# A gated SSM and GEGLU kernel: the sequence transform as 64 by 32 on 64-row TensorE tiles, new scratch layouts, and a fixed order table

## The chip, the cores and the metric

One core of a Trainium2 chip. The metric is device microseconds for one execution. Medians are over all runs of a kernel, ratios over its fast-state runs alone. A "span" is the length of the one execution that was profiled; it is about 2 us below the time. A run is called slow, and left out of the ratios, when it is over 1.5% above the fastest of its kernel. In the profiles PE is TensorE, PEld its weight loads, DVE the vector engine, ACT the scalar engine, POOL GpSimd, SP the engine that issues the transfers and SPq its queue; L851 is line 851 of the kernel in question.

## The reference

Input u is [1, 2048, 640] in bf16. The output mixes a long convolution with a feed-forward network (FFN) by a gate per position:

```python
# branch A: for each of 640 channels a filter K of 2048 taps from 128 complex modes, applied by FFT
P = exp(dt*A * l);  K = einsum("dn,dnl,dn->dl", C, P, dt*B).real
Yf = rfft(pad(u)) * rfft(pad(K));  a = irfft(Yf)[..., :2048] + u * Dskip
# branch B
b = (gelu(x @ w_gate) * (x @ w_up)) @ w_down        # 640 -> 1728 -> 640
g = sigmoid((x * gate_w).sum(-1))
return g * a + (1 - g) * b
```

## The kernel before

The 640 channels are worked in two halves, 0 and 1, of W = 320. For each half the kernel makes tables of the modes (sines on ACT, products on DVE), contracts them to K (TensorE), writes K to DRAM (`dS`), gathers it back (`Kl`), and runs a two-step transform of K and of u, with a trip through DRAM between the steps (`dU`, `dKA`). Spectra are multiplied, transformed back (`dY`), and the last step meets the FFN's result (`zt`).

A complex product needs a second copy `Us` of the spectrum `U`, with real and imaginary rows exchanged. The partitions 0 to 63 hold the real rows, so the exchange is two transfers of contiguous halves:

```python
arena = mp.tile([128, ARENA // 2], BF16, name="arena")     # ONE SBUF tensor for nearly everything;
v = arena[:, off // 2:(off + size) // 2]                   # every buffer is a view of it
...
def u_spec(h, R):
    for c in range(4):
        ks = stageB(dU[h], ..., U[c], ...)
        for s in range(2):
            dma(320, lambda c=c, s=s: nc.sync.dma_start(out=Us[c][64*s:64*s+64], in_=U[c][64-64*s:128-64*s]), r=ks, ...)
def chain(h, R):
    for c in range(4):
        ...                                                # K spectrum -> t
        ve(... U[c]  = U[c]  * t)
        ve(... Us[c] = Us[c] * t)
```

Work is recorded as steps with the data that they read and write; a list scheduler (`plan.run()`) picks engine and order from a cost model. Every engine then has its own list in that order. The waits between engines are not written in the kernel: the recording layer adds them, from the areas that the instructions touch.

Of the kernel before, what the change touches and what calls it, by code (L numbers as in the profile page):

```python
# [12 lines left out]
I32 = mybir.dt.int32  # L13
# [8 lines left out]
X2 = [1, 2, 3, 4, 5, 6, 7, 8, 258, 260, 262, 264, 516, 520, 772, 776, 1032, 1288, 1544, 1800]  # L22
NE = len(X2)


class Plan:
# [50 lines left out]
    def run(self):  # L77
        S = self.steps
        left = [len(s["deps"]) for s in S]
        succ = [[] for _ in S]  # L80
        for s in S:
            for d in s["deps"]:
                succ[d].append(s["i"])
        free, done, aset, line = {}, {}, None, 0
        cand = {}
        ready = {}
        pairs = [0.0] * 4
        owner = {}
        last = None
        warm, cols, wend = False, 0, 3413  # L90

        def arrive(i):
            s = S[i]
            for e in s["engs"]:
                t = 0
                for d in s["deps"]:
                    same = S[d]["eng"] == e and not S[d]["x"]
                    t = max(t, done[d] + (0 if same else S[d]["lat"]))
                ready[i, e] = t
                cand.setdefault(e, set()).add(i)  # L100

        for s in S:
            if not s["deps"]:
                arrive(s["i"])
        order = []
        INF = 1e18
        while len(order) < len(S):
            best = None
            for e, c in cand.items():
                if not c:  # L110
                    continue
                pmin = min(pairs) if e == "PE" else 0
                m = min((max(ready[i, e], pmin) if S[i]["psum"] else ready[i, e]) for i in c)
                t = max(m, free.get(e, 0))
                if best is None or t < best[0]:
                    best = (t, e, pmin)
            t, e, pmin = best
            assert t < INF, "deadlock"
            pick = None
            for i in cand[e]:  # L120
                s = S[i]
                rd = max(ready[i, e], pmin) if s["psum"] else ready[i, e]
                if rd > t:
                    continue
                sc = s["rank"] - s["age"] * (t - ready[i, e]) / 1000
                if s["aset"] not in (None, aset) and e == "ACT":
                    sc += self.switch
                if pick is None or (sc, i) < pick:
                    pick = (sc, i)
            s = S[pick[1]]  # L130
            i = s["i"]
            for e2 in s["engs"]:
                cand[e2].discard(i)
            s["eng"] = e
            s["t"] = t
            ns = s["engs"][e]
            if e == "ACT" and s["aset"] not in (None, aset):
                ns += 1280
                aset = s["aset"]
            if e == "DVE" and last in s["deps"]:  # L140
                ns += 60
            if e == "DVE":
                last = i
            if s["psum"]:
                p = min(range(4), key=lambda q: (pairs[q], q))
                s["k"] = 2 * p
                pairs[p] = INF
                owner[i] = p
            if e == "PE":
                while t >= wend:  # L150
                    warm = cols >= 3072
                    cols = 0
                    wend += 3413
                    if t >= wend + 3413:
                        warm, wend = False, t - t % 3413 + 3413
                rest, ns = ns, 0
                while rest > 0:
                    rate = 1 if warm else 0.5
                    room = wend - t - ns
                    step = min(rest, room * rate)  # L160
                    cols += s["cr"] * step
                    rest -= step
                    ns += step / rate
                    if rest > 0:
                        warm, cols, wend = cols >= 3072, 0, wend + 3413
            free[e] = done[i] = t + ns
            if s["x"]:
                line = max(line, t + ns) + s["x"]
                done[i] = line
            if s["frees"] is not None:  # L170
                f = S[s["frees"]]
                if all(d in done for d in f["rel"]):
                    pairs[owner[f["i"]]] = max(done[d] for d in f["rel"]) + 150
            order.append(s)
            for d in succ[i]:
                left[d] -= 1
                if not left[d]:
                    arrive(d)
        self.order = sorted(order, key=lambda s: (s["t"], s["i"]))
        self.done = done  # L180
        return max(done.values())

    def emit(self):
        for s in self.order:
            s["fn"](s)
# [3 lines left out]
def kernel(  # L189
# [26 lines left out]
    out3 = out.rearrange("b (m p) d -> (b m) p d", p=NPH)  # L216
# [5 lines left out]
    ARENA = 212224  # L222
    arena = mp.tile([128, ARENA // 2], BF16, name="arena")
    ps = pp.tile([128, 8, 512], FP32, name="ps")
    P = dict(sw=5.4, gate=1.91, up=2.5, gelu=8.59, age=0.75, mul=-0.94, un=1.65, uw=1.85, K0=2.33, K1=5.9,
             W=6.08, RT=6.44, ua=0.33, ue=6.48, down=2.99, z=2.89, T2=2.96, A0=6.55, U0=-3.8, A1=2.03, C0=-4.3,
             F0=0.78, U1=1.3, C1=1.89, F1=0.8)
    plan = Plan(P["sw"])
    add = plan.add
# [30 lines left out]
    def mm(n):  # L260
        return n / 2.4 + 4
# [10 lines left out]
    def dma(kb, fn, r=(), w=(), rank=5.0, **k):  # L272
        return add({"SP": 450}, lambda s: fn(), r, w, rank=rank, lat=1900, x=max(100, kb * 3.2), **k)
# [31 lines left out]
    O_TB = O_W + 5120  # L305
    O_WA = O_TB + 768
    O_CS1 = O_WA + 8192
    O_CS2 = O_CS1 + 40960
    O_TRIG = O_CS2 + 25600
    O_PH = O_TRIG + 10240  # L310
    O_A = O_PH + 20480
    O_TAIL = O_A + 8960
# [6 lines left out]
    Wg = [at(O_W + 1280 * k, [128, NKT, 128], BF16, f"Wg{k}") for k in range(2)]  # L319
    Wu = [at(O_W + 2560 + 1280 * k, [128, NKT, 128], BF16, f"Wu{k}") for k in range(2)]  # L320
    TB = at(O_TB, [128, 3, 128], BF16, "TB")
# [16 lines left out]
    vrdt = at(O_TAIL, [N, D], BF16, "vrdt")  # L338
    drow = at(O_TAIL + 1280, [128, D], BF16, "drow")[0:1]
    krow = [drow[:, W * h:W * h + W] for h in range(2)]  # L340
    kst = at(O_TAIL + 2560, [128, 32, 80], BF16, "kst")
    un = at(O_TAIL + 7680, [128, D], BF16, "un")
    ua = [at(O_TAIL + 8960 + 2560 * k, [128, 2, D], BF16, f"ua{k}") for k in range(2)]
    O_TT = O_ZA
    tph = at(O_TT, [128, 2, 512], I32, "tph")
    tsn = at(O_TT + 4096, [128, 2, 512], BF16, "tsn")
    iot = at(O_TT + 6144, [128, 640], I32, "iot")
    tpb = at(O_TT + 8704, [128, 3, 128], I32, "tpb")
# [5 lines left out]
    i4 = cp.tile([128, 4], I32, name="i4")  # L354
    mA = cp.tile([128, 4], FP32, name="mA")
    mQ = cp.tile([128, 4], FP32, name="mQ")
# [8 lines left out]
    dU = [dp.tile([32, 128, W], BF16, name=f"dU{h}") for h in range(2)]  # L365
    dS = [dp.tile([NS, W], BF16, name=f"dS{h}") for h in range(2)]
    dKA = [dp.tile([32, 128, W], BF16, name=f"dKA{h}") for h in range(2)]
    dY = [dp.tile([32, 128, W], BF16, name=f"dY{h}") for h in range(2)]


    kI = iot[:, 0:32]
    tI = iot[:, 32:48]
    k2I = iot[:, 48:112]
    pI = iot[:, 112:240]
    rI = iot[:, 240:368]

    def iotas():
        g = nc.gpsimd
        g.iota(row_i[:], pattern=[[0, 1]], base=0, channel_multiplier=1)
        g.iota(i4[:], pattern=[[1, 4]], base=0, channel_multiplier=0)  # L380
        g.iota(kI, pattern=[[32, 32]], base=8, channel_multiplier=0)
        g.iota(tI, pattern=[[1, 16]], base=0, channel_multiplier=16)
        g.iota(k2I, pattern=[[1, 64]], base=0, channel_multiplier=0)
        g.iota(pI, pattern=[[1, 16], [0, 2], [16, 4]], base=0, channel_multiplier=0)
        g.iota(rI, pattern=[[0, 16], [16384, 2], [0, 4]], base=0, channel_multiplier=0)
        g.memset(ones[:], 1.0)

    pool(2500, iotas, w=["iot", "ones", "ci"])
    jI = tpb.rearrange("p a b -> p (a b)")

    FIELDS = ((0, 3), (5, 31), (0, 31), (3, 31), (2, 1), (0, 63), (6, 1))

    def fields():
        v = nc.vector
        v.memset(b_eps[:], 1e-37)
        for c, (sh, mask) in enumerate(FIELDS):
            v.tensor_scalar(out=fi[:, c:c + 1], in0=row_i[:], scalar1=sh, scalar2=mask, op0=ALU.logical_shift_right,
# [33 lines left out]
    for pl in range(4):  # L431
        ve(v2(1024), lambda pl=pl: expandA(pl), r=["tsn", "fld"], w=[("WA", pl)], rank=RT)
# [278 lines left out]
    def kgen(h):  # L711
        for g in range(4):
            exps1(h, 4 * g, 4)
# [262 lines left out]
```

## Time and profile before

| | before |
|---|---|
| time, median | 345.7 us when the prediction was made, 347.2 with its later runs (344.2 to 349.3) |
| span of the profile | 344.3 us |
| half 0's tables ready (contraction starts) | 101.4 us |
| half 1's tables ready | 183.2 us |
| from there to the end | 161.2 us, 228 GB/s |

The prediction shows the lines for this. Two groups that it only names matter below: the transforms of K and u (line 851) and back (line 880). Columns after the bar: busy us, mean ns of one, idle time before them and what ended it.

```profile
L851 PE MATMUL ps<-arena 128*128 128x320 bf16 x128 | 22.6, 310 | 5.6 <-DMA arena<-dU 3.0 <-DMA arena<-dKA 1.4 <-ACT arena L289 0.4
L880 PE MATMUL ps<-arena 128*128 128x320 bf16 x128 | 18.7, 299 | 0.0
```

### The profile page before, as it was taken

To read this page: it belongs to the slowest core of one execution; us is meant where nothing else is said; L and a number is where in the kernel's file an instruction comes from. 1 tells how busy PE (TensorE), PEld (TensorE's weight loads), DVE (VectorE), ACT (ScalarE), POOL (GpSimd) and SP (SyncE) were. 2 spreads that over 40 slices of the span, in tenths; PEclk is the share of its full clock that TensorE was granted. 3 is DMA by queue.
4 is the path that set the end of the run, shared out by engine and by line. 5 is a ranking of instruction groups with operands and counts; after the bars stand their busy time and mean duration, and the time that the engine had idled before them with its cause. 6 is when DMAs were issued, how large, how long until landed. Compare 5 with 4: busy or idle time off the path is not lost.

```text
span 344.3 us, 6849 instructions
## 1 busy us (share of the span) xinstructions
PE 273.3 (79%) x2785; PEld 155.4 (45%) x2798; DVE 238.2 (69%) x331; ACT 220.5 (64%) x302; POOL 4.0 (1%) x15
## 2 busy tenths in 40 slices
PE   0289999988994699999995267439699999899953
PEld 0044444433673367544443243214346666566731
DVE  5969887999894258698973044524649865799364
ACT  4999986996894499788995046534547853525200
POOL 3000000000000000000000000000000000000000
PEclk9999999999998589999998569858989999999995
DMA  7972222455543223453256529757999799996495
GB/s 242 343 247 57 77 78 76 134 171 151 155 116 101 66 34 76 131 182 83 76 146 136 105 38 216 167 166 176 307 344 351 243 295 305 256 345 204 165 321 163
DMA packets 57989, 60.66 MB, mean 176 GB/s; under 512 B 9475, under 2 KB 53318, under 8 KB 57926
## 3 DMA queue, kind: packets, MB, share of 16 engines
q1 hardware_dynamic: 57958, 60.23, 61.1%
q8 instruction: 22, 0.36, 0.4%
q14 instruction: 9, 0.07, 0.1%
HBM read 35.80 MB, written 19.17 MB: 160 GB/s over the span
## 4 chain that ended last, share of the span: by engine, by line
PE 49%; DMA 25%; SPq 9%; issue 8%; DVE 4%; ACT 2%; DVEq 0%; ACTq 0%
PE ps L530 16%; PE ps L578 12%; PE ps L550 10%; DMA arena<-dY 8%; PE ps L880 4%; SPq L707 3%; PE ps L678 3%; DMA arena<-dKA 3%; ACT arena L289 2%; DMA arena<-in_params_dram 2%; DMA arena<-in_w_gu_dram 2%; DMA arena<-dU 2%; PE ps L748 2%; DMA arena<-in_u_nat_dram 2%; DMA dKA<-arena 2%
## 5 line engine op out<-in xcount | busy, mean ns | idle before, releaser
L289 ACT CAST arena<-ps 128x640 bf16<-128x640 f32 (+2 forms) x110 | 69.4, 692 | 65.8 <-DVE arena L293 26.1
L530 PE MATMUL ps<-arena 128*128 128x512 bf16 x274 | 65.0, 388 | 16.9 <-DMA arena<-in_w_gu_dram 16.0
L550 PE MATMUL ps<-arena 128*128 128x512 bf16 x253 | 63.1, 397 | 13.8 <-DMA arena<-in_w_gu_dram 10.3
L293 DVE CAST arena<-ps 128x640 bf16<-128x640 f32 (+2 forms) x62 | 48.4, 800 | 36.6 <-PE ps L678 21.7
L578 PE MATMUL ps<-arena 128*128 128x320 bf16 x448 | 65.2, 306 | 0.5 <-ACT arena L289 0.3
L578 PEld LDWEIGHTS <-arena 128*128 128x128 bf16 x448 | 44.6, 100 | 19.6 <-issue 1.3
L530 PEld LDWEIGHTS <-arena 128*128 128x128 bf16 x280 | 27.6, 99 | 50.6 <-DMA arena<-in_w_gu_dram 16.0
L550 PEld LDWEIGHTS <-arena 128*128 128x128 bf16 x260 | 26.2, 101 | 46.9 <-DMA arena<-in_w_gu_dram 11.7
L554 DVE TENSOR_TENSOR arena<-ps,arena 128x1024 bf16<-128x1024 f32 x26 | 31.7, 1219 | 18.6 <-PE ps L550 16.2
L618 ACT ACTIVATE arena<-arena 128x2560 bf16<-128x2560 int16 x18 | 41.6, 2340 | 1.6 <-DVE arena L614 1.5
L534 ACT ACTIVATE arena<-ps 128x1024 bf16<-128x1024 f32 (+1 forms) x28 | 27.1, 1024 | 7.6 <-PE ps L530 7.4
L678 PE MATMUL ps<-arena 128*20 128x32 bf16 x1280 | 12.7, 198 | 18.6 <-issue 18.6
L851 PE MATMUL ps<-arena 128*128 128x320 bf16 x128 | 22.6, 310 | 5.6 <-DMA arena<-dU 3.0
L639 DVE TENSOR_TENSOR arena<-arena 128x2560 bf16<-128x2560 bf16 x16 | 23.0, 1484 | 3.8 <-ACT arena L618 3.8
L628 ACT ACTIVATE arena<-arena 128x320 bf16<-128x320 f32 x64 | 23.2, 454 | 0.9 <-DVE arena L481 0.9
L678 PEld LDWEIGHTS <-arena 128*20 128x20 bf16 x1280 | 11.3, 99 | 20.3 <-issue 20.3
L295 DVE TENSOR_SCALAR arena<-ps,omg 128x640 bf16<-128x640 f32 x9 | 7.9, 882 | 18.0 <-PE ps L578 17.9
L851 PEld LDWEIGHTS <-arena 128*128 128x128 bf16 x128 | 12.5, 101 | 14.7 <-DMA arena<-dU 3.8
L880 PE MATMUL ps<-arena 128*128 128x320 bf16 x128 | 18.7, 299 | 0.0
L904 DVE SCALAR_TENSOR_TENSOR arena<-ps,g_f,arena 128x320 bf16<-128x320 f32 x32 | 15.4, 544 | 2.7 <-PE ps L898 2.7
L666 DVE TENSOR_TENSOR arena<-arena 128x2560 bf16<-128x2560 bf16 x10 | 14.9, 1486 | 3.2 <-ACT arena L618 3.1
L612 DVE SCALAR_TENSOR_TENSOR arena<-arena 128x320 int32<-128x320 f32 x40 | 16.9, 483 | 0.0
(89 smaller groups left out, 225.2 us busy)
## 6 DMA issues: line engine op xcount, KB each, us to landing
arena<-in_w_gu_dram SPq DMA_DIRECT2D x52, 160.0 KB
dU<-arena SPq DMA_DIRECT2D x32, 160.0 KB
arena<-dU SPq DMA_DIRECT2D x8, 640.0 KB
arena<-arena SPq DMA_DIRECT2D x16, 320.0 KB
dKA<-arena SPq DMA_DIRECT2D x8, 640.0 KB
arena<-dKA SPq DMA_DIRECT2D x8, 640.0 KB
dY<-arena SPq DMA_DIRECT2D x8, 640.0 KB
arena<-dY SPq DMA_DIRECT2D x8, 640.0 KB
```

What stands on the lines that cost most here:

```text
L289: nc.scalar.copy(out=dst, in_=src(b))
L293: nc.vector.tensor_copy(out=dst, in_=src(b))
L530: nc.tensor.matmul(ps[:, k + j, :], lhsT=Wg[w][:, kt, :], rhs=xT[2 * grp + j][:, kt, :], start=(kt == 0), stop=(kt == NKT - 1))
L534: add({"ACT": an(1024)}, lambda s: nc.scalar.activation(out=HTall[0:p, :, f, :], in_=ps[0:p, plan.bank(g):plan.bank(g) + 2, :], func=ACT.G ...
L550: nc.tensor.matmul(ps[:, k + j, :], lhsT=Wu[w][:, kt, :], rhs=xT[2 * grp + j][:, kt, :], start=(kt == 0), stop=(kt == NKT - 1))
L554: add({"DVE": v1(1024)}, lambda s: nc.vector.tensor_tensor(out=HTall[:, :, f, :], in0=ps[:, plan.bank(u):plan.bank(u) + 2, :], in1=HTall[: ...
L578: nc.tensor.matmul(ps[:, k + h, 0:W], lhsT=HTq[q][:, f, 128 * j:128 * j + 128], rhs=Wd[f][:, W * h:W * h + W], start=(f == 0), stop=(f == ...
L618: ac(an(2 * n * W), lambda: nc.scalar.activation(out=t[:], in_=ph.bitcast(I16)[:, :, :, 0:32:2], func=ACT.Sin, scale=SIN_SCALE), r=[f"ph{k ...
L628: nc.scalar.activation(out=cs1[:, 1, :, 4 * s:4 * s + 4], in_=quads(aT[:, ds]), func=ACT.Exp, scale=float(sg * (4 + 8 * i)))
L678: nc.tensor.matmul(ps[32 * cg:32 * cg + NE, k + b, 32 * i:32 * i + 32], lhsT=cs2[:, q, c, cg:4 * NE:4], rhs=cs1[:, q, c, cg:128:4], start= ...
L851: nc.tensor.matmul(ps[:, k + b, 0:W], lhsT=TB[:, 0, :], rhs=bi[s][:, 2 * a + b, :], start=True, stop=True)
L880: nc.tensor.matmul(ps[:, k + b, 0:W], lhsT=TB[:, m, :], rhs=x[:, 2 * a + b, :], start=(m == 1), stop=(m == 2))
```

## The change

Its intent: half the multiplications of the transform (64-row tiles, four at a time in the array), a K contraction with full weights and few instructions, four K writes in place of twenty, and half 0's whole chain among the FFN and half 1's tables, so that transfers and engines are loaded together. The order comes from a fixed table of 975 entries instead of the scheduler. The core of the diff:

```diff
+ORDER = [int(v) for v in """ 12 6316 276 336 ... """.split()]      # step, engine and PSUM pair of all 975 steps
-    plan.run()
     plan.emit()
 # contraction, per half: 640 matmuls of 32 columns -> 160 of 80 columns, and 16 that select
-    nc.tensor.matmul(ps[32*cg:32*cg+NE, ...], lhsT=cs2[:, q, c, cg:4*NE:4], rhs=cs1[:, q, c, cg:128:4], ...)
+    nc.tensor.matmul(ps[:, ...], lhsT=cs1[:, x, k0+i, :], rhs=cs2[:, x, k0+i, :], ...)
 # transform: one 128-row matmul -> 64-row, 64-column tiles
-    nc.tensor.matmul(ps[:, k+b, 0:W], lhsT=TB[:, 0, :], rhs=bi[s][:, 2*a+b, :], ...)
+    for y in range(2):
+        for x in range(2):
+            nc.tensor.matmul(ps[64*y:64*y+64, k+x, 0:W], lhsT=TB[64*x:64*x+64, 0, :], rhs=t[64*x:64*x+64, 2*a+y, :], ...)
 # real and imaginary rows now alternate, so the exchange takes every second partition
-    nc.sync.dma_start(out=Us[c][64*s:64*s+64], in_=U[c][64-64*s:128-64*s])
+    nc.sync.dma_start(out=Us[s:128:2], in_=U[1-s:128:2])
 # FFN down weights are loaded a second time: half 0's chain uses their place in between
+    wd_load(P["wd"])
```

(Not shown: layouts of the DRAM scratch, the 18 gathers, the setup tables, the costs for the scheduler.)

## The prediction

> **What bounds the kernel now.** I read the page's busy line first: no engine is the bound for the whole span.
>
> ```profile
> PE 273.3 (79%) x2785; PEld 155.4 (45%) x2798; DVE 238.2 (69%) x331; ACT 220.5 (64%) x302; POOL 4.0 (1%) x15
> ```
>
> So I cut the span at the K-table matmuls (line 678), which separate its phases, and asked for each engine's busy time in each stretch. The columns are: stretch, its length, busy us of PE, PEld, DVE, ACT and POOL (instructions in brackets), granted PE clock, DMA share, GB/s.
>
> ```profile
> 15.00:101.40 86.40, 81.47 (x470) 40.72 (x476) 77.36 (x105) 76.70 (x89) 0.00 (x0) 1.00 0.45 128
> 101.40:117.70 16.30, 8.32 (x650) 6.42 (x650) 6.93 (x15) 6.75 (x9) 0.00 (x0) 0.72 0.33 95
> 117.70:183.15 65.45, 64.59 (x355) 34.67 (x359) 50.02 (x60) 59.95 (x84) 0.00 (x0) 0.97 0.40 104
> 183.15:201.92 18.77, 6.17 (x642) 5.67 (x642) 2.61 (x3) 3.29 (x5) 0.60 (x1) 0.61 0.45 95
> 201.92:248.00 46.08, 30.76 (x146) 15.12 (x148) 23.06 (x27) 23.32 (x30) 0.00 (x0) 0.83 0.76 187
> 248.00:300.00 52.00, 47.20 (x306) 30.10 (x307) 36.79 (x38) 30.16 (x48) 0.00 (x0) 0.97 0.97 300
> 300.00:321.90 21.90, 21.40 (x152) 14.56 (x151) 20.21 (x27) 9.87 (x15) 0.00 (x0) 1.00 0.81 260
> 321.90:344.30 22.40, 13.36 (x86) 8.13 (x84) 10.52 (x20) 0.00 (x0) 0.00 (x0) 0.84 0.75 225
> ```
>
> The reader is to see four regimes. Up to 183 us three engines are loaded and the DMA engines are over half idle. The two contractions (101 to 118, 183 to 202) leave everything nearly idle. After 202 everything waits for transfers: 35.0 MB (GB/s times length, summed over the last four rows) in 142 us, 245 GB/s. The end is a ladder of waits. The chain of waits names them (start, us, what):
>
> ```profile
> 183.15 1.45 PE ps L678 x141
> 184.60 2.14 issue
> 186.74 1.24 PE ps L678 x123
> 187.98 5.23 issue
> ...
> 275.14 7.86 DMA arena<-dU
> 282.99 9.39 DMA arena<-dKA
> 292.39 14.44 DMA arena<-dY
> ```
>
> "issue" is no wait for data: 123 tiny matmuls take 1.24 us, then PE has nothing to run for 2 to 5 us. In the timeline half 1's first K gather is issued at 229.20, 27 us after its contraction, because twenty table writes of 10 to 40 KB stand in the queue between.
>
> [...]
> 1. [...]column tiles: line 678 has four of them, and 123 matmuls in 1.24 us are 10 ns each[...]. Row tiles[...] no line of before shows.
> 2. [...]Before, 80 loads and one-column matmuls of line 589 take 2.14 us, 27 ns a pair[...].
> [...]
> [...]
>
> **The change part by part.**
>
> *Transform on 64-row tiles.* Lines 851 and 880 have 128 matmuls each and line 898 has 64, of 320 columns. Line 578 gives the pitch in a stream, 28 in 3.80 us, 136 ns. So before: 320 x 0.136 = 43.5 us. After, the first two become 256 each in fours (a quarter of the array each), the third 64 in twos. Ideal: (64 + 64 + 32) x 0.136 = 21.8 us; [...]I estimate 26. Gain about 17 us of PE. PSUM copies stay 640 wide and as many.
>
> *Contraction.* Per half, 640 matmuls become 160 of 80 columns with a 128-column weight. [...]50 x 160 = 8 us, and 1 for sixteen selection matmuls. So 9 us replace 16.3 and 18.8, and with their loads 320 instructions replace 1280 per half, so issue holes should go. It costs copies: 7 of 960 and 2 of 800 per half against 2560 elements before. At 0.8 to 1.0 ns per element (702 and 819 ns for 640), 5440 elements more a half are about 10 us more on ACT and DVE together.
>
> *K table writes.* Twenty of 160-byte runs become four of 640 bytes: sixteen issues at the median 0.64 us, 10 us of queue per half. Gathers go from 15 to 18.
>
> *Long-run layouts.* Before, U and KA are written in 640-byte runs and read in 5120; Y the reverse. After, U and KA are written in 2560 or 5120 and read in 640; Y is written in 640 and read in 5120. The 640-byte packets are as many, 24,576 (three spills of 8192). They move; they do not go. Wd is loaded twice: 2.2 MB more, 62.3 MB in all.
>
> *Setup.* Four phase tables in place of one copied four times: +3 us DVE and +3 ACT early, about -3 and -4 late.
>
> *The order.* The table decodes into one fixed list per engine. Half 0's chain (2.6 MB each of U, swap, KA twice and Y) now lies among the second half of the FFN and half 1's tables. All U of half 1 are ready before its K arrives. I counted each engine's work between milestones of that list with durations from the trace (DVE 0.77 a copy, ACT 0.65, 2.29 a sine, 1.28 a table load, 2.16 a ten-matmul FFN group, 3.80 a down projection), in us:
>
> - to half 0's tables: PE 78, DVE 90, ACT 91
> - to half 1's tables: PE 79, DVE 78, ACT 87
> - to the end: PE 83, DVE 76, ACT 49, DMA 29.4 MB
>
> Total PE 242, DVE 247, ACT 227.
>
> **The sum.** First stage: before it took 101.4 us with 88 us of DVE and 87 of ACT, 87% loaded; 91/0.87 = 104. Second: before, from 117.70 to 183.15, PE ran 99% and ACT 92%. ACT now leads with 87 us; at 90%, 97. Half 1's tables are thus ready at 201, later than 183, because half 0's copies come first. Third: 29.4 MB at 290 GB/s (between 245 and 300) are 101 us. To this I add some of the last ladder, where transfers cannot fill the engines: before it took 22.4 us from the last Y write to the end at 225 GB/s, so about 5. This gives 106, against 161 before. 201 + 106 = 307; I say 308. The gain of 37 is 55 in the last stage less 18 of work moved ahead.
>
> **The rivals.**
> 1. *Nothing is gained by moving:* ACT and DVE stall each other in the first two stages, as both are over 85% loaded and the order is fixed. Against: 87% was reached before. For: the order has many short dependent transfers at two buffers. At 80% load the tables are ready at 222 and the time is 328.
> 2. *DMA latency keeps the last stage:* half 1 still goes contraction, table write, gather, KA write and read, Y write and read. If the 245 GB/s of before stay, stage three is 120 us and the time 321.
> 3. *Tiles do not overlap across row groups,*[...]. Then 256 + 256 + 64 matmuls at 136 ns are 78 us, 52 more than planned; with a third of it hidden in DMA waits, about 340.
> 4. *Better:* if the order fits the chip, load reaches 93% everywhere and the DMA runs at 310 GB/s: 98 + 94 + 98 = 290.
>
> I hold 1 and 2 in part for likely, 3 for unlikely (one in ten), 4 for possible (one in six).
>
> **Range and chances.** Predicted 308 us. Rivals 2 and 4 nearly bound it: 293 to 325 eight times in ten. Faster by over 2% means under 338.8; only row tiles in series with the stalls of rival 1 reach that: 0.94 faster, 0.04 the same, 0.02 slower.
>
> **What would show it.** In the changed profile: the four issue holes of the contraction gone, and about 9 us each; four 64-row matmuls starting within a few ns and a step of four every 140 to 170 ns; DMA share in the middle of the span up from 0.4 to 0.55 or more; the last stage, from half 1's contraction, at 100 to 115 us with PE busy over 75% of it; DVE the busiest of DVE and ACT at about 247. I am wrong if half 1's contraction starts after 215 us, if a step of four takes over 250 ns, or if the last stage is over 125 us.

## The result, and the profile after

| | before | after |
|---|---|---|
| time, median of 4 | 347.2 us | 359.5 us (357.8 to 359.7) |
| half 0's tables ready | 101.4 us | 106.7 us (predicted 104) |
| half 1's tables ready | 183.2 us | 217.3 us (predicted 201) |
| from there to the end | 161.2 us | 140.2 us (predicted 106) |

The ratio is 1.035, with a 95% interval of 1.026 to 1.044. Ratios here are the mean time of one kernel's fast runs over that of the other's of the same rounds, so not quite the ratio of the medians. The change was slower; 308 was predicted.

The page's busy line of the changed kernel, and its three stages (stretch, length, busy us and instructions of PE, PEld, DVE, ACT, POOL, granted clock, DMA share, GB/s):

```profile
PE 269.2 (75%) x2108; PEld 145.2 (41%) x2126; DVE 247.7 (69%) x356; ACT 226.7 (63%) x308; POOL 6.0 (2%) x19
```

```profile
0.00:106.70 106.70, 83.49 (x475) 42.33 (x482) 90.27 (x149) 93.13 (x122) 3.25 (x16) 0.98 0.50 155
106.70:217.30 110.60, 85.19 (x662) 46.35 (x668) 78.70 (x106) 85.64 (x118) 0.00 (x0) 0.94 0.52 156
217.30:357.50 140.20, 100.50 (x973) 56.55 (x978) 78.68 (x103) 47.92 (x69) 2.72 (x3) 0.84 0.69 207
```

The work is what was counted: DVE 247.7 us against 247, ACT 226.7 against 227, and stage by stage 90/79/79 on DVE and 93/86/48 on ACT. What failed is the load: in stage two ACT is busy for 85.64 of 110.60 us (77%, predicted 90%), and in stage three the transfers run at 207 GB/s (predicted 290). Something keeps engines and transfers waiting. The waits on transfers within SBUF (`arena<-arena`, which only the exchange is) say where; columns: us in total, times, longest:

```profile
ACT arena L245 <- DMA arena<-arena: 16.7, 2, 12.9
DVE arena L639 <- DMA arena<-arena: 10.9, 2, 8.0
DVE arena L249 <- DMA arena<-arena: 9.7, 2, 7.5
ACT L888 <- DMA arena<-arena: 9.6, 1, 9.6
DVE arena L886 <- DMA arena<-arena: 7.6, 1, 7.6
```

Now hold these lines against the source. What an exchange reads and writes is used by the copies that fill `U`, by line 820, the product that overwrites `U`, by line 821, the one on `Us`, and by the matmuls that read both. Line 639 is the product for half 1's K tables. Lines 886 and 888 make the table for the last step. Lines 245 and 249 are helpers for all PSUM copies; by their destinations in the built program, the four that wait so are of half 1's K and not of `U`. None of these reads or writes a byte that the exchange moves. DVE's timeline shows one of them (start, us, what, then idle time before it and what ended it):

```profile
206.22 1.48 DVE L639 TENSOR_TENSOR arena<-arena 128x2560 bf16<-128x2560 bf16 x1
215.74 1.49 DVE L639 TENSOR_TENSOR arena<-arena 128x2560 bf16<-128x2560 bf16 x1 [8.05 <-DMA arena<-arena]
217.15 1.22 DVE L526 TENSOR_TENSOR arena<-ps,arena 128x1024 bf16<-128x1024 f32 x1
```

The last table product of half 1 stands for 8.05 us behind an exchange for half 0. Half 1's contraction, which starts at 217.29, waits for it. On the chain that ended last, `DMA arena<-arena` is the largest item (10.8% of the span, some 39 us). Before, no such wait is listed at all.

The instruction list of the built program says the same without any time. Semaphores named DMAHW are transfers:

```
L639 TensorTensor arena<-arena 128x160x16          [waits DMAHW7,DMAHW6]
L639 TensorTensor arena<-arena 128x160x16          [waits DMAHW1,DMAHW0]
L886 TensorScalarPtr arena<-arena,sc 128x1024      [waits DMAHW3,DMAHW4,DMAHW1,DMAHW7,DMAHW0,Pool]
L888 LoadActFuncSet                                [waits DMAHW4,DMAHW3,DMAHW6,DMAHW1,DMAHW7,DMAHW0]
```

And it goes the other way as well. In the transfer queue's own waits, exchanges (line 814) wait for the late sine table's phases and for table products:

```profile
SPq L814 <- DVE arena L886: 7.5, 1, 7.5
SPq L814 <- DVE arena L639: 4.1, 2, 3.9
```

**Theory 1.** A transfer on every second partition of the one big tensor is taken by the recording layer for one that touches much more of it than `U` and `Us`. So it adds waits that no data needs, in both directions, and what stands behind such a wait in the same list comes late with it: after the 8.05 us on DVE above, line 526 starts at 217.15 as the product ends, though the last gelu (line 506) and matmul (line 522) before it had ended by 210.7. **Rivals:** the exchange's true latency, between spectrum and product, holds the queues (1); the fixed table is a bad order (2); the 64-row tiles are slower than thought (3).

### The profile page after: what moved, and what is told of

The parts are those of the page before. It is cut to its first block, busy times and chain, and to the rows that moved or that the text cites. A ratio compares the mean times of both kernels' runs of the same rounds, so it can differ in the third digit from the quotient of the medians.

```text
span 357.5 us, 5587 instructions
## 1 busy us (share of the span) xinstructions
PE 269.2 (75%) x2108; PEld 145.2 (41%) x2126; DVE 247.7 (69%) x356; ACT 226.7 (63%) x308; POOL 6.0 (2%) x19
## 4 chain that ended last, share of the span: by engine, by line
PE 25%; DVE 23%; ACT 12%; DMA 12%; SPq 6%; issue 6%; DVEq 0%; ACTq 0%
DMA arena<-arena 11%; PE ps L550 10%; ACT arena L245 5%; DVE arena L249 5%; PE ps L522 5%; PE ps L502 4%; SPq L746 3%; DVE arena L584 3%; DVE arena L526 3%; DVE arena L854 3%; ACT arena L506 2%; DVE arena L639 2%; ACT arena L629 2%; ACT arena L591 2%; PE ps L782 2%
## 5 line engine op out<-in xcount | busy, mean ns | idle before, releaser
L245 ACT CAST arena<-ps 128x640 bf16<-128x640 f32 (+2 forms) x113 | 74.1, 712 | 64.7 <-PE ps L803 22.4
L502 PE MATMUL ps<-arena 128*128 128x512 bf16 x271 | 67.7, 399 | 20.4 <-DMA arena<-in_u_T_dram 12.5
L249 DVE CAST arena<-ps 128x640 bf16<-128x640 f32 (+2 forms) x65 | 53.4, 862 | 32.2 <-PE ps L782 12.8
L522 PE MATMUL ps<-arena 128*128 128x512 bf16 x251 | 63.0, 401 | 7.0 <-DVE arena L249 3.7
L550 PE MATMUL ps<-arena 128*128 128x320 bf16 x448 | 65.3, 307 | 0.2 <-DVE arena L249 0.2
L550 PEld LDWEIGHTS <-arena 128*128 128x128 bf16 x448 | 44.7, 101 | 19.8 <-issue 1.0
L502 PEld LDWEIGHTS <-arena 128*128 128x128 bf16 x280 | 28.4, 102 | 55.1 <-issue 18.0
L522 PEld LDWEIGHTS <-arena 128*128 128x128 bf16 x260 | 26.1, 102 | 40.0 <-issue 14.5
L782 PE MATMUL ps<-arena 128*128 128x320 bf16 x64 | 13.7, 341 | 20.1 <-DVE arena L249 9.0
L803 PE MATMUL ps<-arena 64*64 64x320 bf16 x256 | 19.3, 341 | 11.0 <-DVE arena L249 6.0
L251 DVE TENSOR_SCALAR arena<-ps,omg 128x640 bf16<-128x640 f32 x12 | 10.6, 882 | 20.8 <-PE ps L550 20.8
L639 DVE TENSOR_TENSOR arena<-arena 128x2560 bf16<-128x2560 bf16 x10 | 14.7, 1483 | 10.9 <-DMA arena<-arena 10.9
L652 PE MATMUL ps<-arena 128*128 128x80 bf16 x320 | 13.2, 207 | 8.9 <-DVE arena L639 6.9
L803 PEld LDWEIGHTS <-arena 64*64 64x64 bf16 x256 | 8.5, 111 | 24.2 <-issue 22.4
L782 PEld LDWEIGHTS <-arena 128*128 128x128 bf16 x64 | 6.4, 105 | 26.7 <-issue 16.5
L721 PE MATMUL ps<-arena 128*128 128x320 bf16 x64 | 12.3, 307 | 6.5 <-ACT arena L506 2.6
L652 PEld LDWEIGHTS <-arena 128*128 128x128 bf16 x320 | 12.7, 103 | 10.2 <-DVE arena L639 6.5
```

What stands on the lines that cost most here:

```text
L245: nc.scalar.copy(out=dst, in_=src(b))
L249: nc.vector.tensor_copy(out=dst, in_=src(b))
L502: nc.tensor.matmul(ps[:, k + j, :], lhsT=Wg[w][:, kt, :], rhs=xT[2 * grp + j][:, kt, :], start=(kt == 0), stop=(kt == NKT - 1))
L522: nc.tensor.matmul(ps[:, k + j, :], lhsT=Wu[w][:, kt, :], rhs=xT[2 * grp + j][:, kt, :], start=(kt == 0), stop=(kt == NKT - 1))
L550: nc.tensor.matmul(ps[:, k + h, 0:W], lhsT=HTq[q][:, f, 128 * j:128 * j + 128], rhs=Wd[f][:, W * h:W * h + W], start=(f == 0), stop=(f == ...
L652: nc.tensor.matmul(ps[:, k + i // g, 80 * (i % g):80 * (i % g) + 80], lhsT=cs1[:, x, k0 + i, :], rhs=cs2[:, x, k0 + i, :], start=(x == 0), ...
```

## The experiments

The medians of the kernel before were 343.6, 348.1, 348.1 and 346.2 us in the four sets (runs 1 to 4, 5 to 8, 9 to 12, 13 and 14). Compare by the ratio to them. Fourteen kernels ran; stages are read from one profiled execution each.

### 1. The tensor cut (right result)

```diff
-arena = mp.tile([128, ARENA // 2], BF16, name="arena")
+CUTS = [20480, 28672, 10240, 17920, 16256, 11520, 40960, 25600, 12800, 20480, 3200, rest]   # bytes per partition
+arenas = [(lo, hi, mp.tile([128, n // 2], BF16, name=f"arena{i}")) for ...]
-v = arena[:, off // 2:(off + size) // 2]
+v = piece(off, size)                      # a view of the tensor in which off lies; same address
```

> The one SBUF tensor that holds everything is cut into twelve tensors at the borders of its regions; same addresses, same instructions, same order, right result. Theory 1 (the half-swapping transfers on every second partition are tracked as if they touched the whole tensor, so phases, K table products and PSUM copies that have nothing to do with them wait for them, and they for those): 320 to 338 us, 20 to 38 less than the changed kernel's 359, the waits of the K table products (10.9 us on DVE) and of the late sine table (7.6 and 9.6 us) on a transfer within SBUF gone, and half 1's contraction starting near 200 instead of 217. Rival 1 (the swap's own latency, between spectrum and product, holds the queues): 355 to 360, same waits moved to the product. Rival 2 (the fixed order itself is bad): 355 to 360.

Measured: 328.0 us, ratio 0.954 (0.947 to 0.960). Not an instruction was added, removed or moved; only waits differ. Stages and DVE's timeline at the same place (line 651 is what line 639 was):

```profile
0.00:110.30 110.30, 86.10 (x476) 42.67 (x483) 90.11 (x149) 93.23 (x122) 3.25 (x16) 0.97 0.48 152
110.30:204.00 93.70, 82.09 (x661) 47.16 (x668) 79.85 (x106) 84.30 (x117) 0.00 (x0) 0.98 0.54 163
204.00:326.00 122.00, 94.47 (x973) 53.79 (x977) 77.49 (x103) 48.21 (x70) 2.71 (x3) 0.92 0.83 252
```

```profile
199.92 2.89 DVE L651 TENSOR_TENSOR arena<-arena,arena 128x2560 bf16<-128x2560 bf16 x2
202.94 1.23 DVE L538 TENSOR_TENSOR arena<-ps,arena 128x1024 bf16<-128x1024 f32 x1
```

The busy times are those of after within a few us, ACT's load in stage two is 84.30/93.70 = 90%, as predicted, and the table products run back to back. Half 1's tables are ready at 204.0 (predicted 201). The waits of table products, late sine table and copies on an exchange are gone from the list; only stage A's weight loads and matmuls still name one. The exchanges (line 826 here) wait for nothing but the copies that make the spectrum, and for a load:

```profile
SPq L826 <- ACT arena L257: 2.6, 6, 0.7
SPq L826 <- DMA arena<-dU: 1.6, 1, 1.6
SPq L826 <- DVE arena L261: 0.5, 1, 0.5
```

Theory 1 holds, and rivals 1 and 2 fall as the main cause: neither latency nor order was touched. Of the 31.5 us between the spans, 13.3 are gained before half 1's contraction and 18.2 after it. The granted clock rose with it, from a mean of 0.914 to 0.953, and PE's busy time fell from 269.2 to 262.7 us; as only waits were changed, that is part of their effect.

### 2. Contiguous halves (wrong result on purpose)

```diff
-nc.sync.dma_start(out=Us[s:128:2], in_=U[1-s:128:2])
+nc.sync.dma_start(out=Us[64*s:64*s+64], in_=U[64-64*s:128-64*s])
```

> The swap moves contiguous halves of the partitions instead of every second one: as many transfers of as many bytes in the same order, wrong result on purpose. Theory 1: within 2% of the cut tensor (320 to 338 us). Rivals 1 and 2: 355 to 360 us. If strided partitions are themselves slow to transfer (rival 1b), this run gains and the cut tensor does not: the median transfer from issue to landing falls below the changed kernel's.

Measured: 339.6 us, ratio 0.978 (0.965 to 0.990), from the two runs that count as fast (334.6, which was profiled, and 339.3); the others, 339.9 and 340.6, count as slow. One tensor again, but the stray waits are gone: the wait lists on DVE, ACT, SP and GpSimd equal those of run 1 entry by entry. So it is the step of two in partitions that makes the waits. But by the ratios some 8 us of the gain are missing, which the expectation did not foresee (the median is just outside its 338). The transfer queue of run 1 and then of this run (packets, MB, share of 16 engines' span), with the exchanges' median us from issue to landing:

```profile
q1 hardware_dynamic: 58918, 62.44, 62.5%
arena<-arena SPq DMA_DIRECT2D x16, 160.0 KB, 3.5
arena<-arena SPq DMA_DIRECT2D x8, 320.0 KB, 6.0
```

```profile
q1 hardware_dynamic: 58918, 62.44, 64.6%
arena<-arena SPq DMA_DIRECT2D x16, 160.0 KB, 3.9
arena<-arena SPq DMA_DIRECT2D x8, 320.0 KB, 7.3
```

The same packets and bytes keep the transfer engines busy for 64.6% of 332.8 us, 215 us, against 62.5% of 326.0, 204 us. In this pair, then, the alternating rows were the better transfer with the worse waits: contiguous halves land later (7.3 against 6.0 us for 320 KB). Why they do is not shown. The expectation's rival 1b falls: in the changed kernel the exchanges landed after 2.5 and 3.7 us, sooner than here.

### 3. No exchange at all (wrong result on purpose)

```diff
-dma(..., nc.sync.dma_start(out=Us[s:128:2], in_=U[1-s:128:2]))
+dma(..., None)          # second product: Us = t * t
```

> All 24 swap transfers are left out and the second product reads the K spectrum twice: wrong result on purpose, 5.2 MB and 24 issues less, everything else in the same order. Theory 1: only a little under the cut tensor, 312 to 332 us, because the true wait on the swap is short. Rival 1: 325 us or less while the cut tensor stays at 355 to 360. Rival 2: 350 or more.

Measured: 319.1 us, ratio 0.925 (0.916 to 0.934), within what Theory 1 expected. With the exchange goes all that it can cost: 359.5 − 319.1, some 40 us by the medians. 31 of them are waits that no data asks for (run 1's gain); about 9 are 5.2 MB, 24 issues and true waits together.

### 4 and 5. The scheduler back in place of the table, with one tensor and with the cut

```diff
-for v in ORDER: ...
+plan.run()              # the list scheduler of the kernel before; run 5 with the cut of run 1 as well
```

> The changed kernel with the order table taken out and the list scheduler of the kernel before put back in its place, one tensor as in the changed kernel. Theory 1: no better than the changed kernel, 355 to 385 us, since the same hidden waits strike an order that does not know them. Rival 2 (the table is what is bad): 320 to 345 us.

> The cut tensor together with the list scheduler of the kernel before in place of the fixed table. Theory 1 (hidden waits are what hurt both orders): falls from 363 to 330 to 348 us, by 15 to 33. What it stands above the cut tensor with the table (328) is what the table is worth; I expect 2 to 20 us. If the table were worth nothing or less, 328 or below.

Measured: 363.1 us, ratio 1.054 (1.048 to 1.060), and 344.1 us, ratio 0.991 (0.980 to 1.002). The table is not what is bad. With true waits alone it is worth the step from 0.991 to 0.954, some 13 us of 346; with the stray ones from 1.054 to 1.035, some 6. The cut takes about 20 us from the scheduler's order too.

### 6. Control: the kernel before, cut in the same way

> Control: the kernel before with its tensor cut in the same way. It has no transfer on every second partition. Theory 1: no change, ratio 0.99 to 1.01. If cutting the tensor helps any program of this kind, for whatever reason, 325 to 338 us.

Measured: 345.2 us, ratio 0.998 (0.990 to 1.006). Cutting the tensor did nothing for this program, which has no partition steps.

### 7. All tiled matmuls twice (right result)

```diff
-for y in range(2):
+for y in (0, 1, 0, 1):         # and so in the transform back and in the last step; on the cut kernel
```

> The cut tensor with every matmul of the 64-row and 64-column tiles issued twice in its group, results the same: 576 more matmuls. If the tiles overlap as predicted (a step of four in 140 to 170 ns): PE busy up by 20 to 32 us, time up by 3 to 18 us, 331 to 346. If tiles run one after the other (the prediction's rival 3): PE busy up by about 78 us and the time by over 30.

Measured: 337.3 us, ratio 0.974 (0.966 to 0.983), against 0.954 with them once. The groups in this run:

```profile
L815 PE MATMUL ps<-arena,arena 64*64 64x320 bf16 x512 | 26.3, 316 | 5.1 <-DMA arena<-dKA 2.1 <-DMA arena<-dU 0.9 <-ACT arena L518 0.8
L839 PE MATMUL ps<-arena,arena 64*64 64x320 bf16 x512 | 21.0, 298 | 0.7 <-DVE arena L833 0.3 <-DVE arena L261 0.3
```

PE's busy time rose from 262.7 to 282.0 us, so 576 further matmuls took 19.3 us or 33 ns each, a little under what was expected. 512 in 21.0 us are a step of four in 164 ns (205 in the first group, which waits more often): four tiles do run at once, and rival 3 falls.

### 8. Half 1's exchanged spectrum made by TensorE (right result)

On the cut kernel. The real and imaginary rows then stand in blocks of 32, so half 0's exchanges become four transfers of 32 partitions in place of two.

```diff
+tpb[:, 64:96] = tpb[:, 0:32]                  # table columns re, im, re: the same table, read from column 32, gives im, re
+nc.tensor.matmul(ps[64*y:64*y+64, k+x, 0:W], lhsT=TB[64*x:64*x+64, 32:96], rhs=t[...])   # and a PSUM copy on ACT
-nc.sync.dma_start(out=Us[s:128:2], in_=U[1-s:128:2])                                     # for half 1
```

> The cut tensor, and half 1's swapped spectrum made by TensorE from a column-rotated table instead of by eight transfers: 2.6 MB and 8 issues fewer, 64 tiled matmuls and 16 PSUM copies on ACT more; half 0's swaps as 32-partition blocks (16 more issues); right result. The last stage is bound by transfers (83% share), so I expect 4 to 9 us less than the cut tensor: 319 to 324. If the last stage is a chain of latencies instead, 326 to 332.

Measured: 334.1 us, ratio 0.964 (0.953 to 0.976): a miss, some 4 us longer than run 1 by the ratios (6 by the medians), with intervals that overlap, and not the expected 4 to 9 shorter. Stage three has 2.6 MB less, yet lasts 129.4 us at 219 GB/s. Its sixteen further copies stand in ACT's queue right behind the spectra, whose loads come late (ACT waits 21.3 us for the spectra's matmuls, 15.2 in run 1). What this suggests is that the last stage is not bound by bytes alone; half 0's other form of exchange is mixed into it, though stage two ends at 203.3 as in run 1.

### 9 and 10. Only one region cut off

```diff
+CUTS = [59392, 17920, rest]       # run 9: half 0's U and Us        run 10: [105088, 40960, rest], half 1's
```

> Only the 17,920-byte region with half 0's spectrum and its swapped copy is made a tensor of its own (three tensors in all). By the waits in the built program the hidden waits are all gone with that. Theory 1: 325 to 331 us, the same as the full cut. If the number of tensors or anything else about the full cut mattered: 335 or more.

> Only the 40,960-byte region with half 1's spectrum and swapped copy is made a tensor of its own. By the waits in the built program, one phase instruction of half 1's tables and the late sine table still wait for swap transfers. Theory 1: between the full cut and the changed kernel, 329 to 345 us; the more of the hidden waits are left, the longer.

Measured: 329.2 us, ratio 0.958 (0.941 to 0.976), and 338.1 us, ratio 0.980 (0.969 to 0.991). A cut around one region, the right one, is enough. In the built program its waits equal those of run 1 entry by entry, so the two are repeats, and the stages of run 9 (106.5, 95.8 and 124.8 us, against 110.3, 93.7 and 122.0) show how far single profiles differ. The one in the other place leaves two of the stray waits that I had picked out, on a phase (3.1 us in its trace) and on the late sine table, and it is slower. Which area the recording layer takes such a transfer for, and why cutting off half 1's region also freed instructions from half 0's exchanges, these runs do not tell.

### 11 and 12. Another order of the transfers in the last stage, on the cut kernel

```diff
# run 11: the 14 second loads of the down weights moved behind stage A's last copies but one
# run 12: and the 18 gathers of half 1's K moved directly behind the K writes
```

> The full cut, with the fourteen second loads of the down-projection weights (2.2 MB) moved in the fixed order from among the K gathers to after half 1's first product of stage A. If the load rate of the transfers sets the last stage, half 1's K spectrum comes 3 to 6 us earlier and the time is 322 to 326; if only the chain of latencies does, 326 to 330; if the projection then waits for its weights, over 330.

> As the run before, and all eighteen gathers of half 1's K stand directly behind the table writes in the transfer queue. If the gathers' place in the queue sets the last stage: 315 to 323 us. If half 0's chain, now behind them, holds TensorE's queue in front of stage A: no gain or a loss, 326 to 335.

Measured: 333.4 us, ratio 0.966 (0.955 to 0.977), and 340.9 us, ratio 0.990 (0.977 to 1.003): both longer than run 9 of the same set (329.2), run 11 by little; stage three lasts 129 and 136 us, counted from the contraction's start (203.4 and 205.1). Run 11 came to the last of its outcomes: stage A's last matmul starts at 259.4 and not at 263.8 as in run 1, but then the down projection waits 9.7 us for its weights. In run 12 TensorE stands 14.0 us in front of a transform of u, waiting for its load, and stage A's last matmul starts at 269.5: half 0's chain stands in front of stage A in TensorE's queue, so what delays its loads delays stage A. Neither new order was better than the table's.

### 13 and 14. Transfers of the last stage left out, on the cut kernel (wrong results on purpose)

```diff
# run 13: the second load of the down weights issues nothing     (2.2 MB, not on the chain until late)
# run 14: half 1's K gathers issue nothing                       (1.3 MB, 18 issues, on the chain)
```

> The full cut, order unchanged, without the second load of the down-projection weights (2.2 MB, 14 issues in the last stage); wrong result on purpose. If the bytes of the last stage set its length (2.2 MB at the 252 GB/s seen there are 8.7 us): 319 to 322. If the chain of waits does: 325 to 329.

> The full cut, order unchanged, without the eighteen gathers of half 1's K rows (1.3 MB, about 11 us of queue time); wrong result on purpose. If contraction, table write, gather and stage A are the chain that sets the last stage: 308 to 318. If half 0's chain in front of stage A on TensorE's queue sets it as well: 320 to 326. If neither: 326 to 329.

Measured: 321.5 us, ratio 0.935 (0.926 to 0.945), and 320.9 us, ratio 0.933 (0.925 to 0.941). The last stage of each (that of run 13, then of run 14):

```profile
204.00:319.40 115.40, 91.58 (x949) 52.04 (x946) 75.39 (x100) 47.70 (x69) 2.71 (x3) 0.93 0.80 241
```

```profile
204.00:320.10 116.10, 93.50 (x975) 53.72 (x971) 77.38 (x102) 47.83 (x70) 2.71 (x3) 0.94 0.81 253
```

Both rows are cut at 204.0. By the trace half 1's contraction starts at 203.7 in run 14, but at 201.7 in run 13, so stage three is 117.7 us in run 13 and 116.4 in run 14, against 122.0 in run 1 and 124.8 in its repeat, run 9. The spans are 6.6 and 5.9 us below run 1's. By bytes at 252 GB/s, 2.2 MB would be 8.7 us and 1.3 MB 5.2. So bytes seem to count, as run 13 ended inside its first outcome; but single profiles of the same program differ by almost 3 us in this stage, and a share per MB does not come out of them. Run 14 ended in the second of its outcomes, at the lower edge. Stage A's last matmul starts there at 252.5, 11.3 us before run 1's 263.8, and only 5.9 us of that reach the end, so the chain of half 1's K alone does not set the stage. How the 16 us that stage three is over its prediction divide between bytes and waits stays open.

## Why the prediction was wrong

- **The step that failed** is in *The sum*: "ACT now leads with 87 us; at 90%, 97" and "29.4 MB at 290 GB/s". Both carry loads over from stretches of the kernel before to the new order, and so assume that an instruction waits for the data that it uses and no more. In the changed kernel it does not. With one tensor for everything and an exchange on every second partition, table products and copies waited for exchanges: the five largest groups of waits on an exchange were all of that kind, 54.5 us together, not all of it on the chain. ACT's load was 77% and the transfers' rate 207 GB/s.
- **How much:** the profiled span is 357.5, the sum of the prediction 307. The stray waits are 31.5 us of the 50.5 (span of run 1 against after). The other 19 are stage one, 110.3 against 104; stage two, 93.7 against 97; and stage three, 122.0 against 106. That last one is the mis-sized term: 30.7 MB at 252 GB/s against 29.4 at 290 and 5 us for the ladder. Its cause stays open (runs 11 to 14).
- **The part list** missed it. It described the exchange by its bytes and dependences and did not mention that its partitions changed from halves to every second one, in the diff's one line on it.
- **Rival 1** came near the numbers (tables at 222, 80% load; measured 217.3 and, in stage two, 77%) by luck, as its reason is wrong: with the stray waits gone ACT reaches the 90% of stage two in the same order.
- **Rival 2** (the 245 GB/s of before stay, stage three takes 120 us) is what is left once the waits are true: 122 us at 252. Its own sum, 321, lies 5 us under run 1's span of 326.0. That its reason, the latency of the chain, makes up the difference is not shown.
- **Rival 3** was rightly held for unlikely: a step of four takes 164 ns in a stream (run 7). But alone, between waits, four take 0.33 us (as at 204.88 in the changed kernel), so the two transforms save less of PE's busy time than the stream pitch says: 32.4 us (19.3 and 13.1, below) against 41.3 before. Of the 17 us of PE that were promised for all three (43.5 less 26, an estimate that no trace showed), 12.8 came: with the last step 7.2 against 11.1 us.

```profile
L803 PE MATMUL ps<-arena 64*64 64x320 bf16 x256 | 19.3, 341 | 11.0 <-DVE arena L249 6.0 <-ACT arena L245 2.3 <-DVE arena L526 1.2
L827 PE MATMUL ps<-arena 64*64 64x320 bf16 x256 | 13.1, 302 | 4.3 <-ACT arena L245 2.8 <-DVE arena L249 0.7 <-ACT arena L506 0.4
L652 PE MATMUL ps<-arena 128*128 128x80 bf16 x320 | 13.2, 207 | 8.9 <-DVE arena L639 6.9 <-ACT arena L245 1.3 <-DVE arena L249 0.6
```

- **Its signs:** two of the three that were to show it wrong came, half 1's contraction after 215 us (217.3) and a last stage over 125 (140.2); the step of four stayed under 250 ns in a stream (164). With the cut both are inside (204.0 and 122.0).
- **Right:** the contraction (13.2 us of PE's busy time for both halves, with 2.7 for the selections 8 per half against 9 predicted; 41 ns a pair, where its author's estimate was 50; and none of PE's idle time there is "issue" any more), the work of DVE and ACT to within a microsecond, the bytes (62.8 MB against 62.3), the first stage within 3 us (106.7; in the later runs of this order 106.3 to 110.3). Its "7 of 960" copies are six of 960 and one of 640; its sum of 5440 counts them so.
- **The intent,** to load transfers and engines together, is not contradicted: with true waits the same program is at 0.954 of the kernel before, though that is the gain of all parts of the change together. What found the fault was the trace held against the source: the trace gave the releaser, and the source said that there was nothing to wait for.

The version that beats both is run 1, or run 9 with a cut around one region: 328 to 329 us with the right result.

## What to carry to other kernels

When a group in the waits names a releaser whose data it does not use, suspect the recorded waits before the order or the hardware, and test it by cutting the tensor at the same addresses: nothing else changes. When predicting a move of work, list for each changed transfer not only bytes and users but the shape of its access on both sides, partitions included, and ask whose waits that shape will make. Before counting on a large gain from overlap, look for waits that are wider than the data: here they cost 31.5 us of a span of 357.5 (run 1).
